# A planned attention and two-mixer kernel: scores handed out in halves, copies open to two engines, weights prepared at other places

## The chip, the cores and the metric

The kernel runs on one core of one Trainium2 chip. The metric is the device time of one execution in microseconds (us), from the chip, as the median of several executions. The profile is one more execution, recorded by the hardware profiler; its span reaches from the first to the last instruction of the program. Engines are named as in the profile: PE is TensorE (matmuls), PEld its weight loads, DVE is VectorE, ACT is ScalarE, POOL is GpSimd, SP is the queue that issues every DMA here.

## The reference

Three stages follow one another, all in float32. The batch is 4, the sequence S = 448, the width 768 = 12 heads of 64.

```python
scores = scale * np.matmul(q, k.transpose(0, 1, 3, 2))      # causal mask, softmax
attn = attn / (np.sum(attn, axis=-1, keepdims=True) + 1e-09)
x = np.matmul(attn, v)                                      # to (4, 448, 768)
...
h = np.maximum(xt @ w_tok1, 0.0) @ w_tok2                   # along the sequence, 448 -> 256 -> 448
u = x + h.transpose(0, 2, 1)
x = u + np.maximum(u @ w_ch1, 0.0) @ w_ch2                  # along the width, 768 -> 1536 -> 768
...
h = np.maximum(x @ w_in, 0.0)                               # 768 -> 1024, two halves u and v
v_n = (v - mu) / np.sqrt(var + 1e-06)
v_s = np.einsum('ts,bsd->btd', w_spatial, v_n) + b_spatial[None, :, None]
out = (u * v_s) @ w_out                                     # 512 -> 768
```

## The kernel before

**Precision.** Most products are made from float32 values split into two parts (`hi` by a cast on ACT, `lo` = value minus `hi` by `lo_part` on DVE or POOL), and each product is three matmuls (`mm3`, lines 261 to 263). The weights arrive as 64-bit words and are narrowed by three DVE operations each (`narrow`, lines 276 to 280, output tile `psw`).

**Attention.** There are 24 pairs of heads, n = 0 to 23, six to a batch. `scores(n)` makes a pair's 16 (or, split, 24) score matmuls into PSUM tiles `pss` as one PE job, over four query chunks (0: 64 rows; 1 to 3: 128 rows, with 192, 320 and 448 keys). DVE masks and takes the minimum of each chunk and head (L419), ACT takes the exponentials (L436), POOL multiplies by the reciprocal of the sums (L453). Then the probabilities are turned: for n < `BLOCKS` by 16 transposes on PE into `pst` with four copies to `PT` (`transposed`, L490 and L494/L496), from `BLOCKS` on by nine DVE transposes and a way through DRAM (`turned`). `weighted(n)` multiplies with `v` into `pso` (L594, L599 or, for turned pairs, L580) and ACT copies the result to `U` (L602). The probabilities of a pair lie in buffers of place `n % 4` while n < `AHEAD`, and of `n % 2` after that; places 2 and 3 are the buffers `h0` to `h5`, which later hold the hidden rows of `ch1`.

**Mixers.** `token_mix` (tiles `psm`) follows each three pairs. `channel(0)` and `channel(1)` run batch 0 and 1 through the channel mixer (tiles `ps`, weights `whl`, inputs `uhl`), between the later pairs. `channel_pair(2, 3)` takes the other two batches at once by seven products in place of eight (`seven`, tiles `psf`), which needs sums and differences of inputs (`factors`, tile `fb`, sums in `ts`, `hs`, `U`) and of weights (`weight_factors`, `split_weights`, tiles `raw` and `fa`). Later come the gate halves (`psf` again, results `gate`), the value halves (`value`, tiles `psv`, weights `value_w` from `wf`), the product along the sequence (`spatial`, tiles `psp`) and the projection (`project`). `gated_weights` narrows the second mixer's weights during the attention and parks them in DRAM.

**Order.** No order is written by hand. Each piece of work is a `Job` with an engine, a cost in us, a priority and a due time; `Plan.order` lists the jobs by a planned start, and each engine executes its jobs strictly in that order. `START`, `STEP`, `EAGER`, `LEAD`, `SLOPE`, `GATED`, `AHEAD_OF_USE` and others set priorities and due times only. Tables such as `OUT_DVE` and `NORMED_DVE` say which `lo` parts DVE makes; the rest is POOL's.

## Time and profile before

| quantity | value |
|---|---|
| median of three executions | 768.61 us (766.74 to 771.38) |
| the profiled execution, its own time | 769.46 us |
| its span | 767.7 us |
| PE busy | 745.0 us, 97% |
| DVE busy | 629.2 us, 82% |
| ACT busy | 432.3 us, 56% |
| POOL busy | 268.6 us, 35% |
| granted clock of PE over the span | 0.997 |

Busy shares are averages over stretches with different limits. PE counts as busy from a matmul's start to its modelled end, and matmuls overlap, so that 448 columns take about 0.206 us in a row but show as 0.366 us each.

### The profile page before, as it was taken

What the parts mean: (1) busy time and instruction counts of PE and PEld (TensorE: products, weight loads), DVE (VectorE), ACT (ScalarE), POOL (GpSimd) and SP (SyncE); (2) the same over time, 40 slices, a digit from 0 to 9 for tenths busy, and PEclk for the clock granted to TensorE, in tenths of its full rate; (3) what the DMA queues carried; (4) which work ended last, traced back from release to release, by engine and by line L of the source; (5) the groups of instructions that cost most, each with busy time, mean ns of one, the idle gap of its engine ahead of it and who ended that gap; (6) DMA issues with size and microseconds to landing.
All of it is one profiled execution on the core that took longest, in us unless ns stands there. A gap on an engine that the chain in (4) does not pass through costs nothing.

```text
span 767.7 us, 12418 instructions
## 1 busy us (share of the span) xinstructions
PE 745.0 (97%) x4204; PEld 637.9 (83%) x4204; DVE 629.2 (82%) x1513; ACT 432.3 (56%) x1050; POOL 268.6 (35%) x339
## 2 busy tenths in 40 slices
PE   6899899999999999999999999999999999999998
PEld 3467677888988988888898999999888888889997
DVE  5899887899878877867469987999999889599782
ACT  5898666563486466452335666554464565554341
POOL 4679644565579456462420000000541030200000
PEclk9999999999999999999999999999999999999999
DMA  7678776688846897889642122321311100401113
GB/s 266 205 242 261 260 240 234 228 288 302 281 140 195 243 344 256 271 242 286 208 131 113 42 83 82 144 83 42 97 42 42 41 2 1 131 0 41 69 48 132
DMA packets 48319, 122.01 MB, mean 159 GB/s; under 512 B 4864, under 2 KB 19840, under 8 KB 47744
## 3 DMA queue, kind: packets, MB, share of 16 engines
q1 hardware_dynamic: 48256, 121.23, 48.1%
q8 instruction: 33, 0.54, 0.3%
q14 instruction: 30, 0.25, 0.1%
HBM read 91.46 MB, written 29.75 MB: 158 GB/s over the span
## 4 chain that ended last, share of the span: by engine, by line
PE 71%; DVE 18%; ACT 5%; DMA 3%; issue 1%; POOL 1%; SPq 0%; DVEq 0%; ACTq 0%
PE psf L261 8%; PE psf L263 8%; PE psf L262 8%; PE ps L261 7%; PE ps L263 7%; PE ps L262 7%; PE pss L411 4%; DVE fb L252 3%; DVE fa L252 3%; ACT P L436 3%; PE pst L490 2%; DVE U L989 2%; PE pso L580 2%; DVE raw L861 2%; PE psm L261 2%; PE psm L263 2%
## 5 line engine op out<-in xcount | busy, mean ns | idle before, releaser
L261 PE MATMUL psf<-fb,fa 128*128 128x448 f32 x420 | 154.6, 368 | 2.7 <-ACT hs L906 1.4
L263 PE MATMUL psf<-fb,fa 128*128 128x448 f32 x420 | 154.1, 367 | 0.1
L262 PE MATMUL psf<-fb,fa 128*128 128x448 f32 x420 | 154.0, 367 | 0.0
L252 POOL TENSOR_TENSOR whl<-whl 128x768 fp32r<-128x768 f32 x45 | 83.2, 1854 | 82.2 <-ACT whl L729 81.3
L453 POOL TENSOR_SCALAR P<-P,stats 128x448 f32<-128x448 f32 (+1 forms) x192 | 88.2, 479 | 57.9 <-DVE stats L445 42.2
L436 ACT ACTIVATE P<-P,stats 128x320 f32<-128x320 f32 (+2 forms) x192 | 96.0, 506 | 7.7 <-DVE stats L419 7.6
L261 PEld LDWEIGHTS psf<-fb,fa 128*128 128x128 f32 x420 | 78.8, 188 | 12.4 <-ACT hs L906 1.7
L263 PEld LDWEIGHTS psf<-fb,fa 128*128 128x128 f32 x420 | 78.9, 188 | 7.5 <-DVE fa L252 0.5
L262 PEld LDWEIGHTS psf<-fb,fa 128*128 128x128 f32 x420 | 78.9, 188 | 7.2
L419 DVE CUSTOM_DVE_ANT_0 P<-pss,mask 128x320 f32<-128x320 f32 (+2 forms) x192 | 69.4, 413 | 14.3 <-PE pss L411 13.6
L848 ACT CAST fa<-raw 128x384 fp32r<-128x384 f32 (+1 forms) x112 | 56.8, 533 | 41.5 <-DVE raw L861 15.8
L252 DVE TENSOR_TENSOR fa<-raw,fa 128x384 fp32r<-128x384 f32 (+1 forms) x109 | 64.5, 616 | 5.8 <-ACT fa L848 5.5
L729 ACT CAST whl<-whl 128x768 fp32r<-128x768 f32 x45 | 37.4, 837 | 45.6 <-DMA whl<-plain 45.6
L252 POOL TENSOR_TENSOR fb<-U,fb 128x448 fp32r<-128x448 f32 x6 | 7.6, 1296 | 147.8 <-ACT fb L812 147.8
L261 PE MATMUL ps<-uhl,whl 128*128 128x448 f32 x144 | 55.0, 382 | 0.0
L261 PE MATMUL ps<-hid,whl 128*128 128x448 f32 x144 | 54.2, 377 | 0.0
L263 PE MATMUL ps<-uhl,whl 128*128 128x448 f32 x144 | 52.7, 366 | 0.0
L263 PE MATMUL ps<-hid,whl 128*128 128x448 f32 x144 | 52.7, 366 | 0.0
L262 PE MATMUL ps<-hid,whl 128*128 128x448 f32 x144 | 52.7, 366 | 0.0
L262 PE MATMUL ps<-uhl,whl 128*128 128x448 f32 x144 | 52.7, 366 | 0.0
L812 ACT CAST fb<-U 128x448 fp32r<-128x448 f32 x57 | 30.0, 566 | 28.5 <-PE pss L411 11.6
L490 PE MATMUL pst<-ident,P 128*128 128x128 f32 x272 | 39.5, 281 | 6.0 <-POOL P L453 3.0
(168 smaller groups left out, 1767.7 us busy)
## 6 DMA issues: line engine op xcount, KB each, us to landing
way<-in_wch SPq DMA_DIRECT2D x24, 768.0 KB, 5.5
whl<-plain SPq DMA_DIRECT2D x45, 384.0 KB, 4.7
stage<-in_qkv SPq DMA_DIRECT2D x24, 448.0 KB, 4.0
plain<-way SPq DMA_DIRECT2D x24, 384.0 KB, 2.9
raw<-plain SPq DMA_DIRECT2D x24, 384.0 KB, 3.5
round<-PB SPq DMA_DIRECT2D x7, 1024.0 KB, 6.9
PT<-round SPq DMA_DIRECT2D x28, 256.0 KB, 5.9
v<-in_qkv SPq DMA_DIRECT2D x24, 256.0 KB, 3.4
```

What stands on the lines that cost most here:

```text
L252: e.tensor_tensor(lo, x, hi.bitcast(F32), op=ALU.subtract)
L261: nc.tensor.matmul(ps, ah, bh, start=(first and i == 0), stop=False, **kw)
L262: nc.tensor.matmul(ps, ah, bl, start=False, stop=False, **kw)
L263: nc.tensor.matmul(ps, al, bh, start=False, stop=(last and i == n - 1), **kw)
L411: nc.tensor.matmul(ps(i, j), a.t[r, q0:q1], c.t[r, ks[j]], start=(k == 0), stop=(k == last))
L419: nc.vector.tensor_tensor_reduce(out=P(i)[:M, j, :], in0=ps(i, j), in1=mask[:M, S - 128 : S - 128 + W] if j == 0 and n < BLOCKS or M == 64 ...
L436: nc.scalar.activation(P(i)[:M, j, :], P(i)[:M, j, :], AF.Exp, bias=s.t[:M, 0, c : c + 1], scale=-1.0, accum_out=s.t[:M, 1, c : c + 1])
L453: nc.gpsimd.tensor_scalar(P(i)[:M, j, :], P(i)[:M, j, :], s.t[:M, 2, c : c + 1], 1.0, op0=ALU.mult, op1=ALU.mult)
L490: nc.tensor.transpose(ps.t[:, c : c + 128], src, ident)
L729: job("ACT", act(DM, False), lambda: nc.scalar.copy(w.t[:, 0, :], w.t[:, 1, :].bitcast(F32)), r=ks, w=ks, prio=p)
L812: job("ACT", act(S, False), lambda: nc.scalar.copy(f(0), x_()), r=wk, w=[(h, k, 0)], prio=p)
L848: job("ACT", act(n, False), lambda: nc.scalar.copy(part(o, 0), at(d)), r=[key(d)], w=[wk], prio=p + 0.1 * o)
```

## The change

Five things are changed. (1) A pair's scores are two PE jobs, chunks 3 and 0, then 2 and 1; the first pair's are three, in the order 0 and 1, then 3, then 2, with chunks 0 and 1 in PSUM banks of their own. (2) The copies of `PT`, of `U` after the attention and of three of the seven products' results carry a second offer (`other`): the planner gives them to ACT or to DVE, whichever it plans to start first. (3) The factors of the first channel weights of `channel_pair` get buffers of their own, in place of those that are in use when the attention ends. (4) The six value weights are split once, when they are parked, and kept in DRAM as two parts (`gatedv`), so that the later load needs no ACT cast and no POOL subtraction; the second mixer's weights use a second buffer from piece 16 on. (5) Numbers: `AHEAD` 10 to 12, `BLOCKS` 17 to 16, fewer `lo` parts on DVE in the last stage (`OUT_DVE`, `NORMED_DVE`), and other due times and priorities.

```diff
-AHEAD = 10
-
-EAGER, START, STEP = 12, 105.0, 16.4
+AHEAD = 12
+
+EAGER, START, STEP = 12, 112.0, 16.5
...
-OUT_DVE = tuple(range(7))
-
-VALUE_DVE = ()
-NORMED_DVE = (1, 2, 3)
+OUT_DVE = (2, 3, 5, 6)
+
+NORMED_DVE = (1,)
...
-GATED = 6.0, 0.3
+GATED = 9.0, 0.6
 GATED_AT = 160.0, 7.0
+
+GATED_U0 = 16
...
-AHEAD_OF_USE = 12.0
-LEAD, SLOPE = 12.0, 2.0
-
-BLOCKS = 17
+AHEAD_OF_USE = 6.0
+LEAD, SLOPE = 14.0, 1.8
+
+BLOCKS = 16
...
+        def add(j):
+            for e in (j.eng, j.other[0]) if j.other else (j.eng,):
+                avail[e].append(j)
...
+            s, j, e = best
+            avail[j.eng].remove(j)
+            if j.other:
+                avail[j.other[0]].remove(j)
+                if e != j.eng:
+                    j.eng, j.us, j.emit = j.other
...
-    PLACE = {3: (0, 0), 0: (0, S), 2: (1, 0), 1: (1, 320)}
+    PLACES = [{0: (2, 0), 1: (2, 64), 3: (0, 0), 2: (1, 0)}, {3: (0, 0), 0: (0, S), 2: (1, 0), 1: (1, 320)}]
...
-        pkeys = [(banks[j][k], 0) for j in range(2) for k in range(2)]
-        job("PE", 2.5 if whole else 1.95, mms, r=split_keys, w=[*pkeys, ("scored", n)], touch=holds, prio=n, at=nominal(n))
+        for some, us in (((3, 0), 1.3 if whole else 1.05), ((2, 1), 1.2 if whole else 0.9)) if n else (((0, 1), 0.9), ((3,), 1.0), ((2,), 0.7)):
+            pkeys = {(banks[j][PLACE[i][0]], 0) for i in some for j in range(2)}
+            job("PE", us, lambda some=some: mms(some), r=split_keys, w=[*pkeys, ("scored", n, some[0])], touch=holds, prio=n, at=nominal(n))
...
-            if n >= 2 * NP and g in (0, 2):
-                job("DVE", dve(N), lambda g=g, ps=ps, N=N: nc.vector.tensor_copy(part(g), ps.t[:, :N]), r=[(ps, 0)], w=[(t, g)], prio=prio_of(n))
-            else:
-                job("ACT", act(N), lambda g=g, ps=ps, N=N: nc.scalar.copy(part(g), ps.t[:, :N]), r=[(ps, 0)], w=[(t, g)], prio=prio_of(n))
+            other = "DVE", dve(N), lambda g=g, ps=ps, N=N: nc.vector.tensor_copy(part(g), ps.t[:, :N])
+            job("ACT", act(N), lambda g=g, ps=ps, N=N: nc.scalar.copy(part(g), ps.t[:, :N]), r=[(ps, 0)], w=[(t, g)], prio=prio_of(n), other=other)
...
+            w = [[buf(t, [2, 2, HALF], F32R, "fa") for t in ts] for ts in (("P0", "P1", "A1", "v1"), ("w2", "w3", "e", "hid"))]
...
-            t, at, key = raw_blocks(f"w{turn[0] % 2}", rows)
+            t, at, key = raw_blocks(f"w{turn[0] % 2}" if turn[0] else "U0", rows)
...
-        ts = [buf(t, [3, S], F32, "ts") for t in ("P0", "P1", "x0", "x1")]
+        ts = [buf(t, [3, S], F32, "ts") for t in ("x0", "x1")] + [buf("U1", [6, S], F32, "ts")]
...
-        t = buf("e", [3 * FF], U32, "gw")
+        ts = [buf(tag, [3 * FF], U32, "gw") for tag in ("e", "U0")]
...
+                job("ACT", act(FF, False), lambda part=part, whole=whole: nc.scalar.copy(part(0).bitcast(F32R), whole()), r=[(t, 1)], w=[(t, 0)], prio=p)
+                job("POOL", pool(FF), lambda part=part, whole=whole: lo_part(nc.gpsimd, part(1).bitcast(F32R), whole(), part(0)), r=[(t, 1), (t, 0)], w=[(t, 0)], prio=p)
+                job("SP", 0.4, lambda t=t, i=i: nc.sync.dma_start(gated_v[i - 8], t.t[:, : 2 * FF].bitcast(F32)), r=[(t, 0)], w=[("gated", i)], prio=p, size=524288)
...
-        job("SP", 0.4, lambda k=k, w=w: nc.sync.dma_start(w.t, gated_w[8 + k]), r=[("gated", 8 + k)], w=[(w, 0)], prio=LOW + VALUE_PRIO + k, size=262144)
-        job("ACT", act(FF, False), lambda k=k, w=w, h=h: nc.scalar.copy(h.t[:, k % 3, :], w.t), r=[(w, 0)], w=[(h, k, 0)], touch=[l], prio=LOW + VALUE_PRIO + k)
-        e, name, us = (nc.vector, "DVE", dve(FF, False)) if k in VALUE_DVE else (nc.gpsimd, "POOL", pool(FF))
-        job(name, us, lambda k=k, w=w, h=h, l=l, e=e: lo_part(e, l.t[:, k % 3, :], w.t, h.t[:, k % 3, :]), r=[(w, 0), (h, k, 0)], w=[(l, k, 1)], prio=LOW + VALUE_PRIO + k, port=True)
+        for x in range(2):
+            h = value_w[k // 3 * 2 + x]
+            job("SP", 0.4, lambda k=k, x=x, h=h: nc.sync.dma_start(h.t[:, k % 3, :].bitcast(F32), gated_v[k][:, FF * x : FF * x + FF]), r=[("gated", 8 + k)], w=[(h, k, x)], prio=LOW + VALUE_PRIO + k, size=262144)
```

The order moves at three places of which the text below speaks. The first is DVE's row at the program's start, on the first pair's chunks, with the semaphores that each instruction waits for. Before:

```order
L419 ISA P_69,stats_65<-pss,mask 64x64 [waits DVE_49,PE_49,Pool_49]
...
L419 ISA P_69,stats_65<-pss,mask 64x64 [waits PE_49]
...
L419 ISA P_69,stats_65<-pss,mask 128x192
...
L419 ISA P_177,stats_65<-pss,mask 128x320
...
L419 ISA P_177,stats_65<-pss,mask 128x448
```

And of the change:

```order
L433 ISA P_69,stats_65<-pss,mask 64x64 [waits DVE_49,PE_49,Pool_49]
...
L433 ISA P_69,stats_65<-pss,mask 64x64 [waits PE_49]
...
L433 ISA P_69,stats_65<-pss,mask 128x192
...
L433 ISA P_185,stats_65<-pss,mask 128x448 [waits PE_49]
...
L433 ISA P_185,stats_65<-pss,mask 128x320 [waits PE_49]
```

Before, one wait on PE stands ahead of all chunks; in the change chunks 0 and 1, chunk 3 and chunk 2 each have a wait of their own.

The second place is PE's row where the first channel matmul (`ps<-uhl,whl`) stands. Before, 56 `pso` matmuls (seven pairs) stand ahead of it, 128 of `pss`, 128 of `pst` and 64 of `psm`:

```order
L599 MATMUL pso<-PT,v 64x128 x2
L490 MATMUL pst<-ident,P_859 128x128 x2
L490 MATMUL pst<-ident,P_636 128x128
L490 MATMUL pst<-ident,P_878 128x128
L651 MATMUL psm<-ident,U_341 128x128 x3
L490 MATMUL pst<-ident,P_859 128x128
L490 MATMUL pst<-ident,P_878 128x128
L490 MATMUL pst<-ident,P_859 128x128 x2
L651 MATMUL psm<-ident,U_341 128x128 x3
L261 MATMUL ps_1159<-uhl,whl 128x448
```

In the change 80 `pso` matmuls stand ahead of it, 176 of `pss`, 172 of `pst` and 104 of `psm`; the transposes just ahead of it (`P_1049`, `P_1260`, `P_1322`) are those of the eleventh pair:

```order
L504 MATMUL pst<-ident,P_1049 128x128 x2
L504 MATMUL pst<-ident,P_1322 128x128
L504 MATMUL pst<-ident,P_1260 128x128
L606 MATMUL pso<-PT,v 64x448 x2
L611 MATMUL pso<-PT,v 64x384 x2
L611 MATMUL pso<-PT,v 64x256 x2
L611 MATMUL pso<-PT,v 64x128 x2
L504 MATMUL pst<-ident,P_1260 128x128 x2
L504 MATMUL pst<-ident,P_1049 128x128
L504 MATMUL pst<-ident,P_1322 128x128
L270 MATMUL ps_1478<-uhl,whl 128x448
```

So the channel mixer's first matmul moved behind two more pairs' scores, three more pairs' products and the token mixing of the second three pairs.

The third place is POOL's row after the attention, from the last channel weights (`whl`) on. Before:

```order
L252 TENSOR_TENSOR whl<-whl 128x768 x11
L252 TENSOR_TENSOR fb<-U_5444,fb 128x448 x3
L252 TENSOR_TENSOR wv<-wf,wv 128x512 x6
L249 TENSOR_SCALAR xsh<-fb 128x64 x6
L252 TENSOR_TENSOR fa<-raw,fa 128x384
```

And of the change, from the same place and then its end:

```order
L261 TENSOR_TENSOR whl<-whl 128x768 x3
L261 TENSOR_TENSOR fb<-U_5487,fb 128x448 x3
L258 TENSOR_SCALAR xsh<-fb 128x64 x6
...
L261 TENSOR_TENSOR gx<-vn,gx 128x512 x2
L261 TENSOR_TENSOR nhl<-vn,nhl 128x512
...
L261 TENSOR_TENSOR fa<-raw,fa 128x768 x3
L261 TENSOR_TENSOR fb<-gate_6332,fb 128x448 x4
...
L261 TENSOR_TENSOR fb<-gate_6851,fb 128x448 x4
L261 TENSOR_TENSOR fb<-gate_6808,fb 128x448 x2
```

The six subtractions for the value weights left this place, and the last stage got 23 of POOL's subtractions that it had not: 12 of `fb`, 3 of `fa`, 4 of `gx` and 4 of `nhl`.

## Rows read from the trace of the kernel before

**Rows 1.** Windows: stretch, length, each engine's busy us, PE clock, DMA share, GB/s.

```profile
0.00:85.00 85.00, 71.82 (x494) 47.07 (x495) 71.34 (x260) 72.19 (x227) 58.40 (x109) 0.98 0.71 237
20.00:80.00 60.00, 53.26 (x399) 36.27 (x398) 54.48 (x204) 55.31 (x172) 48.75 (x81) 1.00 0.71 233
160.00:400.00 240.00, 240.00 (x1503) 208.03 (x1502) 180.66 (x471) 116.44 (x289) 133.85 (x140) 1.00 0.79 249
400.00:420.00 20.00, 18.65 (x91) 16.69 (x90) 19.90 (x39) 12.49 (x26) 0.00 (x0) 1.00 0.29 108
540.00:560.00 20.00, 19.24 (x93) 17.06 (x92) 19.93 (x30) 8.55 (x22) 10.57 (x8) 1.00 0.43 131
560.00:600.00 40.00, 39.09 (x180) 33.07 (x179) 39.09 (x85) 22.64 (x52) 8.70 (x15) 1.00 0.07 21
600.00:760.00 160.00, 160.00 (x769) 143.60 (x768) 128.02 (x261) 79.32 (x166) 13.80 (x20) 1.00 0.14 48
```

**Rows 2.** Waits of PE: waiter, releaser: us in total, times, longest us.

```profile
PE pst L490 <- POOL P L453: 3.0, 3, 1.3
...
PE psf L261 <- ACT hs L906: 1.4, 1, 1.4
```

**Rows 3.** Timeline, first pair's scores: start, length, engine, what, idle before.

```profile
4.18 2.71 PE L411 MATMUL pss<-stage 64*64 64x64 f32 x16
...
7.03 0.22 DVE L419 CUSTOM_DVE_ANT_0 P<-pss,mask 64x64 f32<-64x64 f32 x1 [5.64 <-PE pss L411]
```

**Rows 4.** Groups by form, PE, 4 to 7.2 us: busy us, mean ns, idle.

```profile
L411 PE MATMUL pss<-stage 64*128 64x192 f32 x4 | 1.0, 603 | 0.0
...
L411 PE MATMUL pss<-stage 64*64 64x64 f32 x4 | 0.5, 338 | 0.0
```

**Rows 5.** Timeline of POOL: multiplications of pairs 0, 9 and 10.

```profile
12.06 3.65 POOL L453 TENSOR_SCALAR P<-P,stats 128x448 f32<-128x448 f32 x8 [8.95 <-ACT wt L317]
...
86.94 3.66 POOL L453 TENSOR_SCALAR P<-P,stats 128x448 f32<-128x448 f32 x8 [5.25 <-DVE stats L445]
...
111.57 3.66 POOL L453 TENSOR_SCALAR P<-P,stats 128x448 f32<-128x448 f32 x8 [4.67 <-DVE stats L445]
```

**Rows 6.** Timeline of PE: the 25th channel matmul.

```profile
108.28 0.45 PE L261 MATMUL ps<-uhl,whl 128*128 128x448 f32 x1
```

**Rows 7.** Chain that ended last, pieces of 225 to 245 us: start, us, what.

```profile
230.37 0.88 PE pst L490 x8
...
231.65 0.21 PE ps L263
...
233.95 1.78 PE pss L411 x24
235.73 0.90 PE pso L594 x4
236.63 1.30 PE pso L599 x12
```

**Rows 8.** The same chain, a turned pair's product, 300 to 330 us.

```profile
309.86 2.21 PE pso L580 x24
```

**Rows 9.** Groups by form, DVE: a narrowing step (20 to 80 us), a `PT` copy.

```profile
L278 DVE SCALAR_TENSOR_TENSOR psw<-way,psw 128x384 uint32<-128x384 uint32 x14 | 7.8, 557 | 0.3
...
L494 DVE COPY PT<-pst 128x448 f32<-128x448 f32 x5 | 3.1, 619 | 1.8 <-PE pst L490 1.8
```

**Rows 10.** Groups by form: DVE, 500 to 540 us; DVE, 540 to 560 us; POOL.

```profile
L252 DVE TENSOR_TENSOR fa<-raw,fa 128x384 fp32r<-128x384 f32 x19 | 10.9, 602 | 0.1
...
L252 DVE TENSOR_TENSOR fa<-raw,fa 128x384 fp32r<-128x384 f32 x11 | 9.1, 845 | 0.0
...
L252 POOL TENSOR_TENSOR wv<-wf,wv 128x512 fp32r<-128x512 f32 x6 | 8.6, 1449 | 9.4 <-ACT wv L1065 7.8 <-issue 1.6
```

**Rows 11.** Groups by form, whole span: a `lo` part on POOL and on DVE.

```profile
L252 POOL TENSOR_TENSOR fb<-U,fb 128x448 fp32r<-128x448 f32 x6 | 7.6, 1296 | 147.8 <-ACT fb L812 147.8
...
L252 DVE TENSOR_TENSOR fb<-gate,fb 128x448 fp32r<-128x448 f32 x28 | 16.7, 618 | 0.7 <-ACT fb L812 0.6
```

More of the change, by code (lines that the diff above doesn't have):

```diff
@@ L83, with __init__ @@
 class Job:
-    def __init__(self, eng, us, emit, prio, at, size, index, port):
+    def __init__(self, eng, us, emit, prio, at, size, index, port, other):
         self.eng, self.us, self.emit, self.prio, self.at, self.size, self.index = eng, us, emit, prio, at, size, index
+        self.other = other
         self.port = port or eng == "POOL"
@@ L100, in buf, with job @@
         return b
-    def job(self, eng, us, emit, r=(), w=(), touch=(), prio=0.0, at=0.0, size=0, port=False):
-        j = Job(eng, us, emit, prio, at, size, len(self.jobs), port)
+    def job(self, eng, us, emit, r=(), w=(), touch=(), prio=0.0, at=0.0, size=0, port=False, other=None):
+        j = Job(eng, us, emit, prio, at, size, len(self.jobs), port, other)
         for k in r:
@@ L144, in order, with start @@
         avail = {e: [] for e in engines}
+        def add(j):
+            for e in (j.eng, j.other[0]) if j.other else (j.eng,):
+                avail[e].append(j)
         for j in self.jobs:
             if j.left == 0:
-                avail[j.eng].append(j)
-        choice = dict.fromkeys(engines)
-        def start(j):
-            s = max(free[j.eng], j.ready, port_free if j.port else 0.0)
+                add(j)
+        def start(j, e):
+            s = max(free[e], j.ready, port_free if j.port else 0.0)
             for b in j.bufs:
@@ L162, in order @@
                     continue
-                starts = [(start(j), j) for j in avail[e]]
+                starts = [(start(j, e), j) for j in avail[e]]
                 first = min(s for s, _ in starts)
@@ L182, in order @@
                 end = dma + 1.9
-            avail[j.eng].remove(j)
             done += 1
@@ L198, in order @@
                 if a.left == 0:
-                    avail[a.eng].append(a)
+                    add(a)
         return sorted(self.jobs, key=lambda j: (j.start, j.index))
@@ L384, in scores @@
         banks = [[bank([2 * j + k], "pss") for k in range(2)] for j in range(2)]
+        PLACE = PLACES[min(n, 1)]
+        if n == 0:
+            for j in range(2):
+                banks[j].append(bank([4 + j], "pss"))
         s = stats[place]
@@ L399, in ps, with mms @@
             return banks[j][k].t[:M, o_ : o_ + W]
-        chunks = (3, 0, 2, 1) if n else range(4)
-        def mms():
-            for i in chunks:
+        chunks = (3, 0, 2, 1) if n else (0, 1, 3, 2)
+        def mms(some):
+            for i in some:
                 q0, q1 = CHUNKS[i]
@@ L601, in weighted @@
         job("PE", 2.55, mms, r=[(v, 0), *((t, g) for g in range(4))], w=[(ps, 0)], prio=n)
-        job("ACT", act(S), lambda: nc.scalar.copy(u.t[:, hp, :], ps.t[:, :S]), r=[(ps, 0)], w=u_keys(n // NP, hp), prio=prio_of(n))
+        other = "DVE", dve(S), lambda: nc.vector.tensor_copy(u.t[:, hp, :], ps.t[:, :S])
+        job("ACT", act(S), lambda: nc.scalar.copy(u.t[:, hp, :], ps.t[:, :S]), r=[(ps, 0)], w=u_keys(n // NP, hp), prio=prio_of(n), other=other)
     wt = [buf(f"t{i}", [1536], F32R, f"wt{i}") for i in range(3)]
@@ L905, in gather @@
         if o in (0, 2, 3):
-            job("ACT", act(S), lambda: nc.scalar.copy(h(), ps.t[:, :S]), r=[(ps, 0)], w=hk, prio=prio)
+            other = "DVE", dve(S), lambda: nc.vector.tensor_copy(h(), ps.t[:, :S])
+            job("ACT", act(S), lambda: nc.scalar.copy(h(), ps.t[:, :S]), r=[(ps, 0)], w=hk, prio=prio, other=other)
         elif o == 6:
@@ L941, in seven @@
                     if z or o > 1:
-                        after.append(("scored", NPAIR - 1))
+                        after.append(("scored", NPAIR - 1, 2))
                     if z and o > 1:
@@ L960, in channel_pair @@
         )
-        hs = [buf(f"U{k}", [6, S], F32, "hs") for k in range(2)] + [buf(t, [3, S], F32, "hs") for t in ("P0", "P1", "x0", "x1")]
+        hs = []
         def h_at(q, r, c, i):
+            if not hs:
+                hs.extend([buf(f"U{k}", [6, S], F32, "hs") for k in range(2)] + [buf(t, [3, S], F32, "hs") for t in ("P0", "P1", "x0", "x1")])
             if q == 0:
```

38 lines of the change are left out of this document (25 added, 13 removed).

## Prediction, written before the result

> **What bounds the kernel now.** I read the windows first, because the mean over the span (PE busy 97%) hides where PE waits. From 160 to 400 us and from 600 to 760 us PE is busy for the whole of both stretches [rows 1]: there only PE work that disappears can save time. PE loses time in four places: 13.2 us of the first 85 (85.00 − 71.82), 1.35 us at 400 to 420, 0.76 us at 540 to 560, 0.91 us at 560 to 600 [rows 1]. The waits of PE say on whom: early on POOL's multiplication of the probabilities; later on ACT's handling of the products' results (`hs`) [rows 2]. In the first stage no single engine is the limit: between 20 and 80 us PE is busy 53.3 us of 60, DVE 54.5, ACT 55.3, POOL 48.8 [rows 1]. In the late losses DVE has no room: 19.90 of 20 us at 400, 19.93 of 20 at 540, 39.09 of 40 after that [rows 1]; the ACT work that PE waits for stands behind DVE's sums.
>
> So the change is priced in four terms: the front of the program, one pair's transposes, the junction at 400 us, and the stretch from 540 us.
>
> **The front, by the time at which the channel mixer can start.** After that moment PE has filler work and, before, hardly waits. So I compare equal amounts of PE work. In the change 24 `pss`, 12 `pst` and 8 `pso` matmuls stand ahead of the first channel matmul that before stand behind the 25th (I count in the order: 152, 160 and 72 ahead of that one before; 176, 172 and 80 in the change; `psm` 104 in both). They cost 1.78 + 1.32 + 2.20 = 5.3 us [rows 7]; the 24 channel matmuls that are missing cost 24 × 0.206 = 4.9 us (0.21 each in the chain, rounded [rows 7]). Equal work, so the yardstick is 108.28 us, the start of the 25th channel matmul before [rows 6]. If the change reaches its first channel matmul sooner, PE is ahead by the difference.
>
> That matmul writes into the buffers of the eleventh pair (n = 10), so it waits for that pair's transposes, which wait for POOL. Before, POOL's multiplication of pair 9 starts at 86.94 and that of pair 10 only at 111.57 [rows 5]: pair 10 shared two buffers with its forerunners. With `AHEAD` 12 it has a place of its own and can follow in step. Nine steps before took (86.94 − 12.06) / 9 = 8.32 us each [rows 5].
>
> *The start.* DVE's first reduction came at 7.03 us, just after all 16 score matmuls (4.18 + 2.71 = 6.89) [rows 3]. Now it waits for chunks 0 and 1 alone, some 0.5 + 1.0 us of these 2.71 [rows 4], so 1.2 us less. DVE and ACT follow one another from there, so I carry 1.2 us on.
>
> *The later copies.* Up to pair 9's reductions DVE gets 7 `PT` copies, 3 `U` copies and 3 more `xs` parts, and 4 narrowing steps fewer: 10 × 0.619 + 3 × 0.557 (taken like a narrowing step) − 4 × 0.557 = 5.6 us [rows 9]. DVE has 5.5 us idle between 20 and 80 [rows 1], part of it unavoidable waiting; I let half of the load through, 2.8 us. Between pair 9 and pair 10 stand 11 narrowing steps, three additions, two `hid` parts, one copy and the pair's eight reductions: the reductions run from 0.22 us for the smallest [rows 3] to about a copy's 0.62, some 3.5 us in all (an estimate), so 17 × about 0.6 + 3.5 = 13.7 us if summed, 11.5 us allowing that consecutive instructions overlap (14 steps of 557 ns show 7.8 us busy, the same as the sum, but copies and reductions start before their forerunner's end). So the step is 11.5 us in place of 8.3.
>
> Sum: 86.94 − 1.2 + 2.8 + 11.5 + 3.7 (multiplication) + 1.0 (transposes and queue) = 104.7 us; the front gains 108.3 − 104.7 = **3.6 us**. Bounds: in step, without DVE's load, 86.94 − 1.2 + 8.3 + 4.7 = 98.7, a gain of 9.6; with all of DVE's 5.6 us late and the start worth nothing, 86.94 + 5.6 + 11.5 + 4.7 = 108.7, a loss of 0.4. ACT loses what DVE gains and is no limit here.
>
> **One pair turned by DVE (`BLOCKS` 16).** 16 transposes leave PE, 2 × 0.88 = **1.8 us** [rows 7]; the product costs 2.21 in the new form against 0.90 + 1.30 [rows 7, 8], nothing. PE is full where the pair stands, so all of it counts. Nine DVE transposes and five DMAs lie in a stretch where DVE idles 59 us of 240 [rows 1]; if they came late, PE would do channel work instead. Bounds 0 and 1.8.
>
> **The junction.** PE lost 1.35 us at 400 to 420 with DVE at 99.5% [rows 1, 2]. In the change 19 weight operations of DVE stand ahead of the first `hs` addition, before 11: eight operations of 0.6 us [rows 10], 4.8 us, move to the attention's end. Three narrowing steps of the second mixer's weights and the last token mixing come closer instead. I take **1.0 us** of 1.35; bounds 1.35 and a loss of 1.5 (the three steps on the path).
>
> **From 540 us.** Six POOL subtractions of 1.449 us ran there, and DVE's `fa` parts took 845 ns in place of 602 [rows 10]: 11 × 0.243 = 2.7 us, in a stretch where DVE is full. Both go. PE lost 0.76 and 0.91 us in the two windows [rows 1]; POOL's three `fb` parts stay, and part of the later loss is the value stage's own. I take **0.7 us** of 1.67; bounds 0 and 1.5. The work reappears before 400 us, where ACT is busy 116 and POOL 134 us of 240 [rows 1]: hidden. If POOL were full there, it would cost 6 × 1.449 = 8.7 us of channel weights' time.
>
> **The last stage.** 23 subtractions go to POOL. By the row of `fb` it takes 1.296 us in place of 0.618 [rows 11]; `gx` and `nhl` like `wv`, 1.449 [rows 10], `fa` by its width some 2.2 (an estimate from the `fb` row): 15.6 + 11.6 + 6.6 = 34 us of POOL in 160, for some 15.8 us off DVE (estimated by width from 0.618). POOL slows DVE's two-input work: 2.7 us for 10.57 us of busy POOL [rows 1, 10], so 34 us cost some 9. DVE then has 128 − 15.8 + 9 = 121 us of 160, and PE stays covered: nothing.
> The Trainium skill's page "SBUF — State Buffer", section "Who interferes with whom", speaks against this part: a DVE instruction with two SBUF inputs and a GpSimd instruction that reads SBUF exclude each other for the whole of an instruction. By that rule up to 34 us of DVE could be blocked, and DVE would come to 146 of 160 us. The slowed `fa` row agrees with the rule's direction; its size, a quarter, says that many pairs of instructions miss each other.
>
> **Sum.** 3.6 + 1.8 + 1.0 + 0.7 = 7.1 us off the profiled execution's own 769.46 us: 762.4. The median of the runs is 0.85 us lower, so against it 768.6 − 7.1 = **761.5 us**.
>
> **Rivals.**
> *In step.* DVE's new copies fill its gaps and the front gains the full 9.6: 768.6 − 9.6 − 3.5 = 755.5. For it: DVE idles 5.5 us. Against: ACT, DVE and POOL were all over 80% busy there [rows 1].
> *Front worth nothing.* DVE takes it all (the 108.7 above), and the gain is the pair and part of the rest: 768.6 − 3 = 765.5; so too if the last stage costs what the front gives. The price of that last one: with DVE at the rule's 146 of 160 us, PE would wait as at 540 us, 0.76 us in 20 with DVE full [rows 1], some 4 us in all, from the point where a project's `fb` part ends after PE reaches it.
> *The channel mixer starves (slower).* Units four to six write into `h3` to `h5`, held by pair 11, whose reductions come another 11.5 us after pair 10's. PE then has three units of 18 matmuls (11.1 us) and some token mixing for that time. If DVE falls one further step of 8.3 us behind, PE waits that long: 768.6 + 8.3 − 3.5 = 773.4. It decides when pair 10's multiplication starts after about 108 us.
> *The offer changes little* (copies that ACT keeps): the order already shows 9 of the 24 `U` copies on DVE, so I give it no chance.
>
> **Chances.** Forecast, 758 to 764.7: 0.48. In step, under 758: 0.18. Worth nothing, 764.8 to 772.4: 0.24. Starved: 0.10. About 0.5% (3.8 us) is what a measurement here can tell from no change; by it faster 0.66, same 0.24, slower 0.10. The range 754 to 769 leaves out the starved case and the rim of two others, some 0.15.
>
> **What would show it.** In the changed profile the first DVE reduction stands near 5.8 us; POOL's eleventh multiplication near 100; the first channel matmul near 105, at least before 108.3; PE's loss in the first 105 us below 15 us; no loss of over 0.5 us in the junction; `fa` parts near 600 ns at 540 to 560 us. I am wrong if the first channel matmul comes after 110 us, if PE waits again between 110 and 160, or if PE shows new waits for POOL's `fb`, `gx` or `nhl` after 600 us.

## The result, and the profile after

The changed kernel took 774.22 us (median of 13 runs, 771.34 to 777.59); the kernel before, on the same chip, 769.25 us (13 runs, 766.74 to 771.55). The ratio is 1.0073, with a 95% interval of 1.0053 to 1.0092: slower by some 5 us, where 761.5 us, a gain of 7, was forecast. The profiled spans are 771.7 us after and 767.7 before.

First the windows of the changed kernel, with the columns of [rows 1]; the five short ones are the program's first stage.

```profile
0.00:85.00 85.00, 75.31 (x518) 49.81 (x519) 73.69 (x264) 71.02 (x222) 60.47 (x113) 0.96 0.67 229
...
160.00:400.00 240.00, 237.44 (x1454) 203.62 (x1454) 185.06 (x469) 119.18 (x291) 144.42 (x144) 1.00 0.83 265
400.00:420.00 20.00, 20.00 (x101) 18.43 (x100) 17.64 (x34) 10.94 (x23) 0.00 (x0) 1.00 0.29 109
540.00:560.00 20.00, 18.68 (x90) 16.63 (x91) 19.93 (x37) 9.77 (x26) 6.46 (x7) 1.00 0.49 158
560.00:600.00 40.00, 39.09 (x182) 33.80 (x181) 38.96 (x84) 23.09 (x52) 6.78 (x11) 1.00 0.07 20
600.00:760.00 160.00, 158.63 (x757) 141.73 (x756) 120.12 (x238) 75.12 (x159) 47.03 (x43) 1.00 0.14 47
...
10.00:12.00 2.00, 0.00 (x0) 0.00 (x0) 1.93 (x6) 0.31 (x1) 1.17 (x2) 0.92 1.02 415
12.00:14.00 2.00, 0.75 (x3) 0.46 (x4) 1.93 (x6) 1.07 (x4) 2.00 (x6) 0.50 0.65 263
...
16.00:18.00 2.00, 2.00 (x6) 0.51 (x4) 1.25 (x5) 1.73 (x7) 0.40 (x1) 0.50 0.67 280
18.00:20.00 2.00, 2.00 (x18) 1.40 (x16) 1.29 (x5) 1.06 (x4) 0.00 (x0) 0.87 0.00 0
```

The junction at 400 to 420 us is full now. The first 85 us lose 9.7 us where they lost 13.2. But the stretch from 160 to 400, full before, loses 2.56 us, and 600 to 760 loses 1.37. TensorE's granted clock falls to the lower of its two levels (0.50, that is 1.2 GHz instead of 2.4) in the window 10 to 12 us, in which TensorE does nothing, and is back in that of 18 to 20. The trace of before has the lower level too, half as long (15.7 to 19.1 us; here 11.7 to 18.5).

The waits of TensorE after (columns as in [rows 2]):

```profile
PE pst L504 <- POOL P L467: 4.5, 4, 2.2
PE pst L504 <- DVE hid L264: 1.5, 1, 1.5
PE ps L270 <- DVE U L782: 1.5, 2, 1.3
...
PE psp L1299 <- DVE gate L1307: 1.3, 2, 1.0
...
PE psm L270 <- DVE U L710: 1.2, 1, 1.2
PE ps L270 <- ACT gw L1050: 1.1, 1, 1.1
```

The wait for POOL's multiplication rose from 3.0 to 4.5 us [rows 2]. The `U` and `gw` waits stand in the middle of the program, the one for `gate` in the last stage.

POOL's timeline, the multiplications of pairs 0, 6, 7, 9 and 10, answers [rows 5]:

```profile
10.83 3.63 POOL L467 TENSOR_SCALAR P<-P,stats 128x448 f32<-128x448 f32 x8 [7.73 <-DVE stats L459]
...
54.40 3.64 POOL L467 TENSOR_SCALAR P<-P,stats 128x448 f32<-128x448 f32 x8 [1.98 <-DVE stats L459]
71.59 3.63 POOL L467 TENSOR_SCALAR P<-P,stats 128x448 f32<-128x448 f32 x8 [0.36 <-DVE stats L459]
...
87.43 3.63 POOL L467 TENSOR_SCALAR P<-P,stats 128x448 f32<-128x448 f32 x8 [0.44 <-DVE stats L459]
100.33 3.64 POOL L467 TENSOR_SCALAR P<-P,stats 128x448 f32<-128x448 f32 x8 [2.80 <-DVE stats L433]
```

And TensorE's own timeline at three places: pair 7's scores, the row ahead of the first channel matmul, and the mixer's first product.

```profile
58.89 0.47 PE L424 MATMUL pss<-qh 64*128 64x448 f32 x2
...
59.84 0.47 PE L270 MATMUL psm<-wt,hid 128*128 128x448 f32 x1
60.16 0.36 PE L271 MATMUL psm<-wt,hid 128*128 128x448 f32 x1
60.35 0.37 PE L272 MATMUL psm<-wt,hid 128*128 128x448 f32 x1
...
63.60 1.03 PE L504 MATMUL pst<-ident,P 128*128 128x128 f32 x8
64.56 0.41 PE L424 MATMUL pss<-qh 64*128 64x320 f32 x2
...
103.80 1.06 PE L504 MATMUL pst<-ident,P 128*128 128x128 f32 x8 [0.33 <-ACT PT L508]
105.22 0.97 PE L606 MATMUL pso<-PT,v 128*64 128x448 f32 x4 [0.36 <-ACT PT L508]
106.02 1.46 PE L611 MATMUL pso<-PT,v 128*64 128x384 f32 x12
107.42 0.66 PE L504 MATMUL pst<-ident,P 128*128 128x128 f32 x4
107.83 0.45 PE L270 MATMUL ps<-uhl,whl 128*128 128x448 f32 x1
...
408.33 0.37 PE L270 MATMUL psf<-fb,fa 128*128 128x448 f32 x1
```

Three things are to be read here. Pair 7's first half of scores stands at 58.89, then come eighteen token-mixing matmuls and a group of transposes, and the second half only at 64.56. POOL needs all of the pair's sums, so its multiplication starts 17.2 us after pair 6's: the lead that pair 6 had (54.40; 60.3 in the trace of before) is gone. Second, a half of twelve matmuls takes 0.95 us (58.89 to 59.84) where 24 in one run took 1.78 [rows 7]: two halves cost 0.12 us more. The first full-size matmul behind scores takes 0.32 us to the next (59.84 to 60.16), the one after it 0.19. Third, the first channel matmul came at 107.83, only 0.45 us ahead of the yardstick at 108.28 [rows 6].

**Where the time went.** I took, over every TensorE row of both traces, the time from each start to the next, and put it down as work (the mean of that kind of matmul behind its own kind), idle time, the excess where a matmul with 64 rows or 64 columns (`pss`, `pso`) stands next to a full one ("shape"), the excess at half clock, and the rest. A change of shape is counted where one of the three kinds `pss`, `pso` and all others follows another. Microseconds, before / after:

| stretch | work | idle | shape | half clock | rest | time |
|---|---|---|---|---|---|---|
| start to equal work (108.28 / 107.83) | 80.05 / 80.04 | 12.83 / 10.62 | 1.69 / 2.30 | 1.74 / 2.86 | 10.5 / 10.6 | −0.4 |
| from there to the first `psf` | 287.3 / 282.0 | 1.57 / 4.19 | 4.95 / 7.67 | 0 / 0 | 5.3 / 6.7 | +1.4 |
| from there to the end | 349.7 / 353.4 | 3.08 / 3.85 | 0 / 0 | 0 / 0 | 3.5 / 2.1 | +3.1 |

Of the work, 3.7 us (18 `psm` products) only moved from the second line to the third, and 1.6 us are the transposes of the pair that DVE turns now. So for like work the front gained 0.45 us, the middle lost 5.1, the rest gained 0.6: 4.1 us, as the spans say. The middle is the miss: 2.6 us of idle time and 2.7 us of shape changes that were not there. The idle times are gaps in the rows; the other columns hang on what is taken as a normal step. With other choices from the same rows the middle's shape changes cost 1.7 to 2.6 us more than before, and those of the first two lines together 3.3 to 3.9 (3.3 here).

### The profile page after: what moved, and what is told of

Same layout as the page of the kernel before. It is cut to its first block, busy times and chain, and to the rows that moved or that the text cites. A ratio compares the mean times of both kernels' runs of the same rounds, so it can differ in the third digit from the quotient of the medians.

```text
span 771.7 us, 12447 instructions
## 1 busy us (share of the span) xinstructions
PE 748.0 (97%) x4196; PEld 637.8 (83%) x4196; DVE 634.7 (82%) x1512; ACT 423.8 (55%) x1033; POOL 301.2 (39%) x364
## 5 line engine op out<-in xcount | busy, mean ns | idle before, releaser
L450 ACT ACTIVATE P<-P,stats 128x448 f32<-128x448 f32 (+2 forms) x192 | 95.8, 504 | 25.0 <-DVE stats L433 24.9
L433 DVE CUSTOM_DVE_ANT_0 P<-pss,mask 128x448 f32<-128x448 f32 (+2 forms) x192 | 70.0, 413 | 15.4 <-PE pss L424 15.4
L261 POOL TENSOR_TENSOR ql<-stage,qh 128x896 fp32r<-128x896 f32 x17 | 36.0, 2116 | 17.3 <-ACT qh L363 11.9
```

Of the source, the lines that this page charges most:

```text
L261: e.tensor_tensor(lo, x, hi.bitcast(F32), op=ALU.subtract)
L433: nc.vector.tensor_tensor_reduce(out=P(i)[:M, j, :], in0=ps(i, j), in1=mask[:M, S - 128 : S - 128 + W] if j == 0 and n < BLOCKS or M == 64 ...
L450: nc.scalar.activation(P(i)[:M, j, :], P(i)[:M, j, :], AF.Exp, bias=s.t[:M, 0, c : c + 1], scale=-1.0, accum_out=s.t[:M, 1, c : c + 1])
```

## The experiments

Ratios are against the kernel before on the same chip, from five rounds each. At first four causes were open: the shape changes that the halves bring, the copies that DVE took over, the new numbers, or an order of before that was fitted and that any new plan spoils.

**One part of the change taken back.**

```diff
-        for some, us in (((3, 0), 1.3 if whole else 1.05), ((2, 1), 1.2 if whole else 0.9)) if n else (((0, 1), 0.9), ((3,), 1.0), ((2,), 0.7)):
+        for some, us in (((3, 0, 2, 1), 2.5 if whole else 1.95),) if n else (((0, 1), 0.9), ((3,), 1.0), ((2,), 0.7)):
```

> The changed kernel with each pair's scores after the first as one PE job again (the first pair keeps its three). Theory S (switches): a matmul that follows one of another height or width of the array costs PE about 0.1 us more, and the halves put 34 more such switches ahead of the first psf matmul (56 + 32 before, 68 + 54 in the change); here 83 stand there (45 + 38), so 3 to 4 us come back: ratio to the kernel before near 1.002, and twelve-matmul runs of pss are gone. Theory N (numbers: the later start of the channel mixer and the new due times cost the time): the numbers stay, so the ratio stays at 1.006 to 1.009. Theory D (DVE is late because of the copies it got): stays too.

777.65 us, 1.0121 [1.0092, 1.0150].

```diff
-        self.other = other
+        self.other = None
```

(and the `PT` copies that were DVE's before are DVE's again.)

> The changed kernel without second offers: the copies of PT, U and the products' results stand on the engines that they had before. Theory D: PE's waits for DVE between 108 and 408 us (U additions, 1.3 and 1.2 us) go and 2 to 4 us come back, ratio near 1.002. Theory S: 64 + 50 switches ahead of the first psf matmul are nearly those of the change (68 + 54), ratio 1.006 to 1.008. Theory N: 1.006 to 1.009.

776.74 us, 1.0111 [1.0077, 1.0145].

```diff
-AHEAD = 12
+AHEAD = 10
...
-BLOCKS = 16
+BLOCKS = 17
```

(and the other numbers of the diff's head, but for the two tables of the last stage.)

> The changed kernel with the numbers of before: AHEAD 10, START 105, STEP 16.4, GATED, AHEAD_OF_USE, LEAD, SLOPE and BLOCKS 17; the mechanisms (halves, offers, other buffers, split value weights, fewer lo parts on DVE) stay. Theory N: the first channel matmul comes near 95 us or earlier and the stretch to the first psf matmul loses nothing, so the ratio is 1.000 or lower, less the one pair's 1.8 us. Theory S: 69 + 46 switches, so the time stays 3 us or more above before, ratio 1.004 to 1.008.

776.88 us, 1.0108 [1.0081, 1.0135].

```diff
-OUT_DVE = (2, 3, 5, 6)
+OUT_DVE = tuple(range(7))
-NORMED_DVE = (1,)
+NORMED_DVE = (1, 2, 3)
```

> The changed kernel with all lo parts of the last stage on DVE again (OUT_DVE and NORMED_DVE as before). PE's two new waits at a spatial product for DVE's gate results (1.35 us at 690 to 697 us) come from POOL holding DVE: if so they go and 1 to 1.5 us come back (ratio 1.005 to 1.006), and DVE's two-input work after 600 us shows no slowed instructions. If DVE had them anyway, nothing changes or DVE is fuller and up to 2 us are lost. Theories S, N and D see no difference here.

773.21 us, 1.0061 [1.0043, 1.0080]; TensorE's wait for `gate` is gone. By the medians the tables cost some 1 us; the intervals overlap.

By their medians three of the four came out 2.5 to 3.4 us slower than the change itself (the intervals of two overlap the change's), where theories S, D and N each wanted one of them faster. Each part taken back makes the planner set a new order, and that order waits elsewhere. With one job, and without offers, TensorE's idle time between the first channel matmul and the first `psf` does go, 0.9 and 0.5 us where the change has 4.2, as theory D said for the offers; but behind that `psf` it idles 8.2 us in both, where the change has 3.9. So I next left the planned order alone and moved one thing in it by hand.

**The order kept, the halves moved.** In the changed kernel the first half of a pair's scores goes back to stand ahead of the second; in the kernel before each pair's scores are split round the next TensorE job.

```diff
-    for j in plan.order():
+    for j in arranged(plan.order()):
         j.emit()
```

> The changed kernel with its planned order left as it is on ACT, DVE, POOL and SP nearly everywhere, except that in TensorE's row the first half of a pair's scores is moved back to stand directly ahead of its second half (17 of the divided pairs; nothing is planned anew). Shape theory: what the middle lost is paid where TensorE goes from 64-row or 64-column matmuls to full ones and back. A half of 12 score matmuls takes 0.96 us where 24 together take 1.78, and the first channel matmul behind scores 0.31 us instead of 0.20, so 0.25 us for each division that is removed: 17 of them give 3 to 4 us, 770 to 771.5 us. Wait theory: the halves cost nothing themselves; the middle lost its time in waits for what was planned at other places, and reductions that now come later add some: 774 to 777 us, with more waits of the transposes for POOL's P.

812.88 us, 1.0574 [1.0541, 1.0606]. Both theories were wrong by far. The waits of this kernel:

```profile
PE pst L568 <- ACT PT L572: 8.3, 6, 2.4
PE pss L488 <- DVE way L353: 8.2, 4, 2.8
```

The order is so tight that scores a few microseconds later cost 26 us of idle time up to the first `psf` (40.6 for 14.8), and the granted clock stands at its lower level for 34 us in place of 7: the cost of a division can't be had by undoing it there.

> The kernel before with its planned order, in which each pair's score job is cut in two and the TensorE job that stood behind it is put between the halves (23 divisions more, nothing planned anew, no other edit). Shape theory: 23 times 0.2 to 0.25 us, 773 to 775 us, with as much more between the first channel matmul and the first matmul of the token mixing's second part, and no new idle time. Wait theory: the divisions cost nothing and give the first reduction its banks earlier: 768 to 770 us.

786.76 us, 1.0238 [1.0207, 1.0268]: three times the loss that the shape theory gave, and mostly not by shapes. Up to the first `psf` there are 38 more shape changes, which by the sums of the table cost 3 to 5 us (about 0.1 us each), the idle time rose from 14.4 to 23.7 us, and the half clock cost over 2 us more. The second halves are late, and what follows them waits.

**The halves alone,** planned anew with the numbers of before:

> The kernel before with the two jobs for a pair's scores alone, planned anew with its own numbers. Shape theory: 12 shape changes more in the front and 20 more in the middle, 3 to 4 us: 772 to 774 us. Planning theory (the numbers of before are fitted to its jobs, and any other set of jobs is planned worse): over 775 us, with idle time of TensorE beyond the 4 us of the changed kernel. If the halves give the planner what they are meant to, below 769 us.

770.90 us, 1.0021 [1.0001, 1.0041]: less than either theory said. Up to the first `psf` this kernel idles 7.2 us against 14.4; its 31 more shape changes cost 2.9 us (0.09 us each), the half clock 1.5 us more, and the rest 1.5 more, so that it is there only 1.3 us sooner. Behind it TensorE waits 3.5 us for DVE's `fa`. So the halves do save waits, and most of it is spent on the way.

**TensorE kept busy in the first hole.** The first try:

```diff
             def mms(g=g, ps=ps):
+                if n == 0 and g == 0:
+                    for _ in range(3):
+                        nc.tensor.matmul(ps.t[:, :448], ident, mask[:, :448], start=True, stop=True)
```

> The changed kernel with three matmuls of the identity with the mask, whose result nothing reads, ahead of the first transposes, where TensorE waits 2.2 us for POOL's multiplication. If that hole is what made the granted clock fall to half from 11.7 to 18.5 us, the low clock is gone or halved and the front gains 1 to 1.7 us: 772.5 to 773.5 us. If the clock falls all the same, 774 to 775 us.

777.33 us, 1.0110 [1.0082, 1.0137]. The try failed by its place: the group `g == 0` isn't the first in TensorE's row, so the matmuls stood behind the wait (14.86 to 18.8 us) and cost 4.1 us themselves. It says nothing on the clock.

**The halves with one of the other parts, and the change without it.** Part three is the first channel weights' factors where the attention ends; part four is the value weights kept as two parts. Every run here with part three also has the second buffer from piece 16 on, which the list of the change has under (4); every run without part three is without that buffer too.

> The kernel before with the halves (as in the run of the halves alone, which took 770.9 us) and with part three of the change: the first channel weights' factors in buffers that come free where the attention ends. The halves alone reached the token mixing's second part 1.3 us sooner than before and lost 5.6 us behind it: 3.6 us of waits at 400 to 440 us, most of them 3.5 us for DVE's fa, and a granted clock of half from 420.4 to 427.2 us. Part theory: those go and the middle stays, 765.5 to 767.5 us, below the kernel before. Planning theory: the middle is planned anew and loses what the junction gives, 769 to 774 us.

771.61 us, 1.0022 [1.0003, 1.0041]: the wait for `fa` goes, and the idle time between the first channel matmul and the first `psf` is 4.2 us where the halves alone had 0.7.

> The kernel before with the halves and with part four alone: the value weights split at 210 to 260 us and kept in DRAM as two parts. Part theory: six copies on ACT and six subtractions on POOL come into the stretch with token mixing, where TensorE then waits for the gw buffer and for ACT, 1 to 2 us, and the stretch at 540 to 560 us gives back up to 0.7: 771 to 773 us. If it costs nothing there, 770 to 771 us.

791.91 us, 1.0290 [1.0262, 1.0319]: 20 us worse than either theory. The waits at 425 to 455 us, and SP's last store of the second mixer's weights in its timeline:

```profile
ACT fa L861 <- DMA gated<-gw: 21.9, 1, 21.9
...
PE psf L270 <- ACT fa L861: 20.3, 1, 20.3
```

```profile
441.28 0.32 SPq L1043 DMA_DIRECT2D gated<-gw  x1
```

All pieces of those weights pass through one buffer, `e`, the last ones every 5.5 to 5.7 us (stores at 430.11, 435.55 and 441.28). Part four holds it longer for six of them (a copy, a subtraction and a store of 512 KB): from the load of the first of the six to that of the next piece 135.4 us pass (229.67 to 365.10), with the halves alone 72.4 (230.49 to 302.90). So the last store is issued at 441.28 instead of 378.35 with the halves alone; the channel weights' factors take over the same buffer and wait for it.

> The changed kernel without part four (value weights kept as one part, split where they are read, as before). Part theory: the waits for ACT's gw copy and the gates in the middle go, 1.1 to 2.6 us: 771.5 to 773 us. Planning theory: 774 to 777 us, as with every other part that was taken back.

775.09 us, 1.0073 [1.0047, 1.0100]: as the change. The wait for ACT's `gw` copy goes; 1.2 us ahead of scores for DVE's `gw` and 1.0 us for ACT's `fa` come.

> The changed kernel without part three (the first channel weights' factors where they were before). Part theory: no token-mixing products stand behind the channel mixer's first matmul, the junction at 400 to 420 us loses 1.4 us or more again: 775 to 778 us. If part three is worth nothing, 774 us.

805.43 us, 1.0463 [1.0436, 1.0489]; TensorE waits 25.8 us for ACT's `fa`, the same chain. So where the weights have no second buffer and the factors no other place, part four costs 21 us against the halves alone, and the change takes 31 us more. The buffer and the place were always left out together, so which of them part four needs is not shown. Neither part brings time by itself.

**Early and late halves, crossed** (part three in all four, numbers of before):

```diff
-        for some, us in (((3, 0), 1.3 if whole else 1.05), ((2, 1), 1.2 if whole else 0.9)):
+        for some, us in (((3, 0), 1.3 if whole else 1.05), ((2, 1), 1.2 if whole else 0.9)) if n < 10 else (((3, 0, 2, 1), 2.5 if whole else 1.95),):
```

> The kernel before with part three alone, every pair's scores one job. With the three runs beside it and the run with halves and part three (771.6 us) this makes a table of two by two: halves for pairs 0 to 9 or not, halves for pairs 10 to 23 or not, part three in each. Ledger theory (halves save waits in the front, where pairs alone stand in the row, and cost shape changes behind it, where no wait is left to save): the loss at 400 to 420 us goes, all else as before, 767 to 768.5 us. Planning theory: 770 us or more, at no fixed place.

> The same with halves for pairs 0 to 9 and one job for each later pair. Ledger theory: the front of the run with all halves (3.5 us sooner at equal TensorE work than before), behind it the shape changes of before (51 instead of 78), 764 to 766 us, faster than both kernels. Planning theory: what one stretch gains another loses, 769 to 774 us.

> The same with one job for pairs 0 to 9 and halves for the later ones. Ledger theory: the front of before, 25 shape changes more behind it at 0.12 us and up to 2 us of pieces and waits that go with them, 771 to 774 us. Planning theory: no order among the four; below 770 us would speak against the ledger.

| | pairs 10 to 23 one job | pairs 10 to 23 halves |
|---|---|---|
| pairs 0 to 9 one job | 769.33, 1.0011 [0.9993, 1.0030] | 780.82, 1.0160 [1.0122, 1.0198] |
| pairs 0 to 9 halves | 777.29, 1.0108 [1.0085, 1.0132] | 771.61, 1.0022 [1.0003, 1.0041] |

If the halves had a fixed worth early and another late, the lower right would be the sum of its neighbours' losses, some 2.6% slower (1.1 + 1.6 − 0.1). It is 0.2% slower. The windows and waits of the two mixed kernels show why; first halves to pair 9 (waits from 200 to 240 us), then halves from pair 10 (waits from 160 to 200 us):

```profile
200.00:240.00 40.00, 32.08 (x154) 27.45 (x153) 31.71 (x58) 12.06 (x20) 19.00 (x12) 0.96 0.78 272
```

```profile
PE ps L272 <- POOL whl L261: 2.9, 3, 1.2
PE ps L270 <- ACT whl L742: 2.7, 1, 2.7
```

```profile
160.00:200.00 40.00, 36.64 (x206) 31.79 (x205) 36.66 (x76) 17.11 (x36) 26.29 (x27) 1.00 0.79 293
...
380.00:400.00 20.00, 17.88 (x94) 16.41 (x93) 17.12 (x28) 10.55 (x20) 6.07 (x4) 1.00 0.30 97
```

```profile
PE pst L501 <- DVE xs L261: 3.1, 1, 3.1
```

One loses 7.9 us at 200 to 240 us, 5.6 of them to channel weights (`whl`) that ACT and POOL bring late; the other 3.4 us at 160 to 200, nearly all to DVE, and 2.1 at 380 to 400. The shape changes alone have a steady price in this table: between first channel matmul and first `psf`, 27 fewer changes (halves to pair 9 against all halves) cost 2.7 to 3.3 us less, 24 more (halves from pair 10 against none) 2.3 to 2.8 us more, by what is taken as a normal step; that is 0.1 to 0.12 us for one.

Then the same in the changed kernel: halves up to pair 9, one job for each later pair.

> The changed kernel with halves for pairs 1 to 9 and one job for each later pair. Ledger theory: 22 shape changes fewer in the middle, 2.8 us: 770.5 to 772 us. Planning theory: as when all halves were taken back (777.65 us), with the same loss behind the first channel-mixer product and idle time of 8 us ahead of it: 775 to 778 us.

780.37 us, 1.0137 [1.0111, 1.0162]: it fails on the changed kernel as planning theory said, with 3.1 us of loss at 400 to 420 us again.

**The hole filled in its place, and the first pair's jobs alone.**

```diff
+                if fill:
+                    for m in (448, 192):
+                        nc.tensor.matmul(ps.t[:, :m], ident, mask[:, :m], start=True, stop=True)
                 for k, (c, src) in enumerate(blocks):
+                    if fill and k == 1:
+                        nc.tensor.matmul(ps.t[:, 128:384], ident, mask[:, :256], start=True, stop=True)
                     nc.tensor.transpose(ps.t[:, c : c + 128], src, ident)
```

> The changed kernel with the hole at 9.9 to 12.1 us filled in its right place this time: two matmuls of the identity with the mask (448 and 192 columns) directly ahead of the first transposes, and one of 256 columns behind the first transpose, where TensorE waits 1.1 us; the transposes overwrite their results, nothing else is edited. In the first try of this kind the matmuls stood behind the wait and took 4.1 us themselves. If the hole is what made the granted clock fall, the clock stays up and the front gains 1 to 2 us: 772 to 773 us, with no stretch at half clock from 11 to 19 us. If the clock follows the whole light front and not this hole, it falls a few us later and the time stays at 774 to 775 us.

772.37 us, 1.0051 [1.0030, 1.0071]. The interval overlaps that of the change, so the time alone doesn't decide; the trace does. Windows, then TensorE's and POOL's timeline of this kernel:

```profile
10.00:12.00 2.00, 1.75 (x10) 0.86 (x6) 1.88 (x6) 0.47 (x2) 1.25 (x3) 1.00 1.02 412
12.00:14.00 2.00, 1.13 (x6) 0.67 (x6) 1.93 (x6) 1.06 (x4) 2.00 (x6) 1.00 0.75 263
...
16.00:18.00 2.00, 2.00 (x20) 1.38 (x20) 1.93 (x6) 2.00 (x9) 0.32 (x1) 1.00 0.61 252
```

```profile
10.41 1.34 PE L508 MATMUL pst<-mask,ident 128*128 128x448 f32 x4
...
105.67 0.45 PE L270 MATMUL ps<-uhl,whl 128*128 128x448 f32 x1
```

```profile
52.21 3.65 POOL L467 TENSOR_SCALAR P<-P,stats 128x448 f32<-128x448 f32 x8 [1.95 <-DVE stats L459]
69.40 3.63 POOL L467 TENSOR_SCALAR P<-P,stats 128x448 f32<-128x448 f32 x8 [0.36 <-DVE stats L459]
```

The clock stays at its upper level, and not in this execution alone: over the span all seven of this kernel have a granted clock of 0.999 or 1.000, the thirteen of the change 0.995 to 0.998. Everything behind stands 2.2 us sooner: POOL's pair 6 at 52.21 instead of 54.40, pair 7 at 69.40 instead of 71.59, the first channel matmul at 105.67 instead of 107.83. Pair 7 is still 17.2 us behind pair 6, so the two losses are separate.

> The kernel before with the first pair's three jobs alone (64-row chunk first, banks of its own), planned anew with its own numbers. As the forecast priced it, the first reduction starts 1.3 to 1.5 us sooner and the lead lasts through the pairs that follow: 767 to 768 us. Planning theory: the lead of the first pair is used up within the next few pairs and the rest is planned anew, 769 to 775 us, with new waits behind 85 us.

777.17 us, 1.0119 [1.0098, 1.0141]. Its window at 420 to 440 us:

```profile
420.00:440.00 20.00, 16.67 (x74) 13.07 (x73) 18.99 (x37) 11.88 (x25) 0.00 (x0) 1.00 0.14 43
```

The lead is gone before 85 us (7.6 us of idle time from 25 us to the first channel matmul, 6.2 before), and 3.3 us are lost at a new place, behind the mixer's first products.

## Why the prediction was wrong

**The front: forecast 3.6 us, measured 0.45.** The start was right: the first reduction stood at 5.5 us (forecast 5.8), POOL's first multiplication 1.2 us sooner [rows 5]. Pair 10's multiplication was to start at 100.0 and started at 100.33, but that was luck: pair 9's stood at 87.43 instead of 88.5, and the step from it took 12.9 us instead of 11.5, two errors that nearly cancel. The term that failed is the last one, "1.0 (transposes and queue)": from the end of the multiplication at 103.97 to the first channel matmul it took 3.86 us, because pair 9's product (16 `pso`, 2.2 us) stands in TensorE's row between pair 10's transposes (103.80 and 107.42). That is 2.9 of the 3.15 us, and it could have been read ahead: the order of the change shown above has these products between these transposes. Two losses on the way were not in the sum, and its generous allowances for DVE covered them: the hole at 9.9 to 12.1 us with the half clock behind it cost 2.2 us (shown by filling it), and pair 7 lost the lead of pair 6, since its second half of scores stands 5.7 us behind the first (read from the timeline, not tried by itself).

**One pair turned: 1.8 us forecast.** The work fell by 1.6 us: right, and lost again in the same stretch.

**The middle: nothing forecast beyond that pair, 6.7 us lost** (5.1 and the pair's 1.6). The step that failed is the sentence that from 160 to 400 us "only PE work that disappears can save time", together with "After that moment PE has filler work and, before, hardly waits". I took a full TensorE for a property of the stretch. It is one of the order: with another order the same engine waits 2.6 us more there and changes shape 17 times more, 2.7 us by the table. "Hardly waits" also passed over a loss of before, 2.7 us from 85 to 160 us, which is 4.0 after:

```profile
85.00:160.00 75.00, 72.33 (x488) 60.34 (x487) 60.18 (x162) 47.03 (x123) 41.34 (x47) 1.00 0.73 244
...
85.00:160.00 75.00, 71.00 (x479) 57.41 (x478) 66.15 (x175) 43.60 (x117) 36.00 (x49) 1.00 0.71 246
```

The shape changes could have been read before: by the same sums the trace of before spends 5 us on 51 of them in the middle, and the order shows 34 more in the change from start to first `psf` (122 for 88). I counted matmuls, not their neighbours.

**The junction: 1.0 forecast, 1.35 recovered** at 400 to 420 us by the window. But part three alone, with that loss gone, took 769.33 us, no less than before: what it gains there doesn't come through to the time.

**From 540 us: 0.7 forecast, −0.56 measured** (1.32 lost at 540 to 560 instead of 0.76, 0.91 at 560 to 600 as before). The groups by form of DVE at 540 to 560 us answer [rows 10]:

```profile
L261 DVE TENSOR_TENSOR fa<-raw,fa 128x384 fp32r<-128x384 f32 x14 | 8.7, 648 | 0.0
```

`fa` fell from 845 to 648 ns (forecast 600), but DVE stayed full (19.93 of 20): it has 14 of them there instead of 11, and 37 instructions instead of 30. The mean of before hid two kinds: six parts of 0.55 us, and five of 0.98 to 1.52 us that stand beside a POOL subtraction. Such stretching cost DVE 5.5 us of this window before and 1.8 after; so DVE's load, not the slow parts, is the likely loss (read from the rows, not tried).

**The last stage: forecast nothing, about 1 us.** As a sum, DVE's busy time was sized well, 120.1 of 160 us for 121 forecast. The step that failed is "PE stays covered": the sum does not say which instruction comes late. TensorE waits 1.3 us for two `gate` products of DVE. DVE has no idle time ahead of them, but two of its instructions, each with both inputs in SBUF, stand beside a subtraction of POOL. DVE's two, then POOL's:

```profile
690.65 1.91 DVE L261 TENSOR_TENSOR fa<-raw,fa 128x768 fp32r<-128x768 f32 x1
...
693.87 1.55 DVE L830 TENSOR_TENSOR gate<-gate,gate 128x448 f32<-128x448 f32 x1
```

```profile
690.55 1.20 POOL L261 TENSOR_TENSOR fb<-gate,fb 128x448 fp32r<-128x448 f32 x1 [0.86 <-ACT fb L825]
691.70 3.23 POOL L261 TENSOR_TENSOR gx<-vn,gx 128x512 fp32r<-128x512 f32 x2
```

Alone the first takes 0.95 us and the second 0.62; here they end 0.8 and 0.5 us after POOL's. In this stage nine DVE instructions with both inputs in SBUF start after a POOL subtraction and before its end; all nine are stretched so, 6.5 us in all. Six that start ahead of POOL's keep their time, and so do twenty with one input in PSUM. These single instructions agree with the Trainium skill's page "SBUF — State Buffer", section "Who interferes with whom", by which such a pair exclude each other. The 146 us estimated from its rule did not come, since only nine met. With the tables taken back DVE is busier, 130.2 us in the same window, but none of its instructions is stretched near the `gate` products, and the waits are gone.

**Is it the halves, the numbers, or the planning?** Shown is that no part has a price of its own that could be taken back: of the nine kernels with one part undone or one part alone none was faster than before, and the crossed table is not a sum. The ledger, by which halves gain in front and lose behind, fell with that table; of it only the price of a shape change held, as a size of about 0.1 us. The rival that fits all runs is that the planner's order of before is a good one among many, and each new set of jobs or numbers gets another order with waits at other places (200, 160, 380, 420 us). The forecast's slow rival had 773.4 us, near the 774.2 measured, but by luck: its condition, pair 10's multiplication after about 108 us, did not come (100.33). That an order as good exists for the changed jobs was neither shown nor excluded: I tried no search over the numbers. No kernel here beats the one before.

## What to carry to other kernels

When a change alters what a planner may choose from, a full engine before is no promise of a full engine after: price the new order, stretch by stretch, and give replanning a chance of its own that is as large as that of any gain. Count shape changes on TensorE beside matmuls when jobs are cut smaller, and look what comes to stand between the pieces in the row, since the consumer waits for the last one. Beside an engine's busy sum, look which of its instructions can meet another engine's. Before a step holds a shared buffer longer, follow its tag to the next owner.

## What the hardware showed that I had not expected

Each change between matmuls with 64 rows or 64 columns and full ones cost 0.06 to 0.13 us by the sums of this study, by run and by what is taken as a normal step (0.10 in the change, 34 more for 3.3 us), and two halves of scores take 1.90 us instead of 1.78. In a hole of 2.2 us near the start (9.9 to 12.1), with 1.1 us more a moment later, the clock went to its lower level, at 11.7 us until 18.5; three matmuls that nothing reads, put into these holes, kept the upper level throughout and brought all that follows forward by 2.2 us.

A DVE subtraction or sum with both inputs in SBUF that started during a POOL subtraction ended 0.48 or 0.49 us after that one's end, however much of it was left (0.82 us for the one with 768 columns): nine instructions from 600 to 760 us of the change, of which the longest took 1.91 us.
